# Seven block products for eight in the last channel mixing of a linear-attention and mixer kernel

## Chip, cores and metric

The kernel runs on one core of one Trainium2 chip. The metric is device time in microseconds (us) of one execution; the time of a kernel is the median of several runs.

## What is computed

Attention output of eight batches is the input of a token and channel mixer. Cut to what matters:

```python
# q, k, v: (8 batches, 8 heads, 576 positions, 64)
q_p, k_p = phi(q), phi(k)                       # phi(x) = (x if x > 0 else exp(x) - 1) + 1
kv = einsum('bhsd,bhse->bhde', k_p, v)
num = einsum('bhsd,bhde->bhse', q_p, kv)
den = einsum('bhsd,bhd->bhs', q_p, sum(k_p, axis=2))[..., None] + 1e-06
x = (num / den), as (8, 576, 512)
u = x + (relu(x^T @ w_tok1) @ w_tok2)^T         # token mixing: 576 -> 256 -> 576
out = u + relu(u @ w_ch1) @ w_ch2               # channel mixing: 512 -> 1536 -> 512
```

The change touches the last product, `relu(u @ w_ch1) @ w_ch2`, of the last two batches.

## The kernel before

The 576 positions of a batch are four row tiles of 128 (`R = 4`) and a tail of 64; the tails of two batches (a pair `p`, batches n = 2p and 2p + 1) share one tile of 128. A row tile r holds the positions 9p' + 2r + e: the lower 64 partitions are e = 0, the upper 64 are e = 1, and `outv` sends each half to its own rows of the output.

Each batch goes through these steps:

- `phi` on q and k: ScalarE takes the exponential (L124), VectorE adds (L130) and takes a minimum (L138). `kv` and `nd` form the attention; `nd_end` has VectorE divide (L217, L219, L220).
- `mm1` and `mm2` are the token mixing. `mm2` leaves its product in a PSUM tile `h_ps`, and VectorE adds x to give `u` (L271). `mm2_tails` does so for a pair's tail (L280, L284), giving `ut`. DMA transposes make `uT` and `uTt` of them (L464, L469).
- `mm3` is the first half of the channel mixing: 12 blocks of 128 hidden channels, each of 4 matmuls of 512 columns (L480); ScalarE applies the relu and writes block mc of the bf16 tile `cr[n % 2]` (L487). `mm3_tail` does the same for the tails of a pair, 48 matmuls of 128 columns (L494), into `crt`.
- `mm4` is the second half. A row tile t takes 12 matmuls of 512 columns (L506) into one PSUM bank; `mm4_end` has VectorE add `u` into an output tile `o_sb` (L523, or L533 for the tail tile, t = 8) and starts the transfers to the output (L528, L535).

PSUM has two pools: `ps_big` with four banks of 128 x 512 f32 and `ps_sm` with two tiles of two banks. `o_sb` tiles come from a pool of five.

The order on every engine is written out by hand. The main loop runs over n from 2 to 7. Its list `big` holds the steps of `mm3` (0 to 11), for odd n those of `mm3_tail`, then thirds of `mm4` tiles. The list `fill` says which steps of the next batches are put after which step of `big`: the next batch's kv, nd, mm1, mm2a (row tiles 0 and 1), mm2b (2 and 3) and mm2t (tails) come at the places in `AT`. Each engine works through its queue in this order; a step that waits holds everything behind it on its engine.

For the last pair the outputs are sent from the queues of SP and ACT, one row tile at a time, and for the other pairs from POOL's queue, two row tiles at a time:

```python
last = p == B // 2 - 1
put = nc.sync if last else nc.gpsimd
```

The last row tile of batch 7 is done by `mm4_last` in two parts of 384 and 128 columns (L543), so that the last add (L546) and transfers (L548) are short.

Below, batch 6 and batch 7 are n = 6 and n = 7.

Of the kernel before, what the change touches and what calls it, by code (L numbers as in the profile page):

```python
# [9 lines left out]
FP32 = mybir.dt.float32  # L10
BF16 = mybir.dt.bfloat16
AF = mybir.ActivationFunctionType
ALU = mybir.AluOpType
# [5 lines left out]
def kernel(  # L19
# [20 lines left out]
    nc = tc.nc  # L40

    B, H, S, D = q.shape
    DM = H * D
    DTOK = moe_w_tok1.shape[1]
    DCH = moe_w_ch1.shape[1]
    R = 4
# [7 lines left out]
    NCH = DCH // 128  # L54
# [6 lines left out]
    outp = ctx.enter_context(tc.tile_pool(name="outp", bufs=5))  # L61
    ps_big = ctx.enter_context(tc.tile_pool(name="ps_big", bufs=4, space=bass.MemoryType.PSUM))
    ps_sm = ctx.enter_context(tc.tile_pool(name="ps_sm", bufs=2, space=bass.MemoryType.PSUM))

    def const(name, shape, dt=BF16):
        return consts.tile(shape, dt, name=name, tag=name)
# [6 lines left out]
    wc2 = const("wc2", [128, NCH, DM])  # L73
    identity = const("identity", [128, 128])

    raw = {(nm, b): const(f"{nm}_raw{b}", [128, HP, TD], FP32) for nm in "kvq" for b in range(2)}
# [7 lines left out]
    u = [const(f"u{b}", [128, R, DM]) for b in range(2)]  # L84
    ut = [const(f"ut{i}", [128, DM]) for i in range(2)]
    uT = [const(f"uT{b}", [128, R, NDM, 128]) for b in range(2)]
    uTt = const("uTt", [128, NDM, 128])
    cr = [const(f"cr{b}", [128, NCH, SM]) for b in range(2)]
    crt = const("crt", [128, NCH, 128])
# [6 lines left out]
    half = [slice(0, 64), slice(64, 128)]  # L96
# [11 lines left out]
    def load(nm, n, c, gate=None):  # L108
        src_ = src[nm][n].rearrange("(j a) (p t) d -> (a p) j (t d)", a=2, t=T)
        js = slice(2 * c, 2 * c + 2)  # L110
        return after(nc.sync.dma_start(out=raw[nm, n % 2][:, js], in_=src_[:, js]), gate)
# [7 lines left out]
    live = {}  # L119
# [22 lines left out]
    def phi(nm, n, c):  # L142
        phi_exp(nm, n, 2 * c, 2)
        phi_add(nm, n, 2 * c, 2)
        phi_end(nm, n, 2 * c, 2)
# [49 lines left out]
    def qtr_dma(n):  # L195
        for a in range(2):
            nc.sync.dma_start_transpose(
                out=qT[n % 2][:, 2 * TD * a:2 * TD * (a + 1)].rearrange("p (f s) -> p f s", s=D),
                in_=qp[half[a]].rearrange("p c t i d -> p (c t i d)"))
# [274 lines left out]
    def mm3(n, mc, kjs=range(NDM), dve=False):  # L474
        b = n % 2
        if kjs[0] == 0:
            part_of[mc] = ps_big.tile([128, 512], FP32, name="c_ps", tag="big")
        ps = part_of[mc]
        for kj in kjs:
            nc.tensor.matmul(out=ps, lhsT=wc1[:, kj, 128 * mc:128 * mc + 128],  # L480
                             rhs=uT[b][:, :, kj],
                             start=(kj == 0), stop=(kj == NDM - 1))
        if kjs[-1] == NDM - 1 and dve:
            nc.vector.tensor_scalar(out=cr[b][:, mc, :], in0=ps, scalar1=0.0, scalar2=None,
                                    op0=ALU.max)
        elif kjs[-1] == NDM - 1:
            nc.scalar.activation(out=cr[b][:, mc, :], in_=ps, func=AF.Relu)  # L487

    def mm3_tail(i):
        ps = ps_big.tile([128, 4, 128], FP32, name="c_ps", tag="big")  # L490
        for m in range(4):
            mc = 4 * i + m
            for kj in range(NDM):
                nc.tensor.matmul(out=ps[:, m], lhsT=wc1[:, kj, 128 * mc:128 * mc + 128],  # L494
                                 rhs=uTt[:, kj, :], start=(kj == 0), stop=(kj == NDM - 1))
        nc.scalar.activation(out=crt[:, 4 * i:4 * i + 4, :], in_=ps, func=AF.Relu)
# [3 lines left out]
    def mm4(p, t, kcs, wait=False):  # L500
        if kcs[0] == 0:
            held[t] = ps_big.tile([128, DM], FP32, name="h2_ps", tag="big")
        ps = held[t]
        b, r = divmod(t, R)
        for kc in kcs:
            nc.tensor.matmul(  # L506
                out=ps, lhsT=crt[:, kc, :] if t == 8 else cr[b][:, kc, 128 * r:128 * r + 128],
                rhs=wc2[:, kc, :], start=(kc == 0), stop=(kc == NCH - 1))
        if kcs[-1] == NCH - 1 and not wait:
            mm4_end(p, t)  # L510

    outv = out.rearrange("n (p t) d -> n p t d", t=T)
# [23 lines left out]

    def mm4_last(cs):

        p, b, r = B // 2 - 1, 1, R - 1
        m = cs.stop - cs.start  # L540
        ps = ps_big.tile([128, 512], FP32, name="h2_ps", tag="big")[:, 0:m]
        for kc in range(NCH):
            nc.tensor.matmul(out=ps, lhsT=cr[b][:, kc, 128 * r:128 * r + 128],  # L543
                             rhs=wc2[:, kc, cs], start=(kc == 0), stop=(kc == NCH - 1))
        o = outp.tile([128, 2, DM], FP32, name="o_sb", tag="o_sb")[:, 0, 0:m]
        nc.vector.tensor_tensor(out=o, in0=ps, in1=u[b][:, r, cs], op=ALU.add)  # L546
        for e in range(2):
            (nc.scalar if e else nc.sync).dma_start(out=outv[2 * p + b, :, 2 * r + e, cs],  # L548
                                                    in_=o[half[e]])

    def prep_k(n, g, copy=nc.scalar.copy):
        phi("k", n, g)
        vcast(n, g, copy)

    def load_all(n, nms):
        if n < B:
            for nm in nms:
                for g in range(2):
                    load(nm, n, g)
# [118 lines left out]
    def steps(n):  # L678

        out_ = [("kv", lambda: kv(n, range(2)))]  # L680
        if n == 1:
            puts = [nc.scalar.copy, nc.vector.tensor_copy if n == 1 else nc.scalar.copy]
            out_ += [(f"qt{c}", lambda c=c: qtr(n, c, puts[c])) for c in range(2)]
        for i, rs in enumerate(([0, 1], [2, 3], [4])):
            for g in range(2):
                out_.append((f"nd{i}{g}", lambda g=g, rs=rs: nd(n, g, rs)))
        out_.append(("mm1", lambda: mm1(n)))
        if n > 1:
            out_ += [("mm2a", lambda: mm2(n, [0, 1])), ("mm2b", lambda: mm2(n, [2, 3]))]
            if n % 2:  # L690
                out_.append(("mm2t", lambda: mm2_tails(n // 2)))
            out_ += [("uta", lambda: utr_dma(n, [0, 1])), ("utb", lambda: utr_dma(n, [2, 3]))]
            if n % 2:
                out_.append(("utt", lambda: utr_tail_dma(n // 2)))
        return out_

    def run(bigs, fill):
        for i, big in enumerate(bigs):
            big()
            for s, fn in fill:  # L700
                if s == i:
                    fn()
        for s, fn in fill:
            assert s < len(bigs)

    m3 = lambda n, k0=0: [lambda mc=mc: mm3(n, mc) for mc in range(k0, NCH)]
    m3t = [lambda i=i: mm3_tail(i) for i in range(3)]
    m4 = lambda p, ts: [lambda t=t, i=i: mm4(p, t, range(4 * i, 4 * i + 4))
                        for t in ts for i in range(3)]
# [6 lines left out]
    big = [lambda mc=mc: mm3(0, mc, range(2, 4)) for mc in range(3)] + \  # L716
# [4 lines left out]
    fill = [(2, mm2_first_tail)]  # L721
# [8 lines left out]
    first = steps(1)  # L730
# [12 lines left out]
    big = [lambda mc=mc: mm3(1, mc, range(2, 4)) for mc in range(3)] + [lambda mc=mc: mm3(1, mc, dve=mc in (5, 8)) for mc in range(3, NCH)] + m3t + m4(0, [4, 5, 6, 7, 8])  # L743
    at1 = {"kv": 8, "nd00": 10, "nd01": 11, "nd10": 12, "nd11": 13, "nd20": 14, "nd21": 15,
           "mm1": 17, "mm2a": 19, "mm2b": 20, "mm2t": 21, "uta": 19, "utb": 20}
    fill = [(s, lambda g=g: phi("k", 2, g)) for g, s in ((0, 0), (1, 2))]
# [11 lines left out]
    for n in range(2, B):  # L758
        p, b = divmod(n, 2)
        if b == 0:  # L760
            big = m3(n) + m4(p, [0, 1, 2, 3])
        else:
            big = m3(n) + m3t + m4(p, [4, 5, 6, 7, 8])
            if n + 1 == B:
                big = m3(n) + m3t + m4(p, [8, 4, 5, 6]) + [
                    lambda: mm4_last(slice(0, DM - 128)), lambda: mm4_last(slice(DM - 128, DM))]
        fill = []
        if n + 1 < B:
            fill += [((AT3 if n == 2 else AT)[nm], fn) for nm, fn in steps(n + 1)]
        if n + 2 < B:  # L770
            d = 1 if n == 2 else 0
            fill += [(s + d, lambda g=g: phi("q", n + 2, g)) for g, s in ((0, 8), (1, 9))]
            fill += [(12 + d, lambda: qtr_dma(n + 2))]
            if n == 2:
                fill += [(16, lambda: load_all(5, "qkv"))]
            fill += [(s + d, lambda g=g: prep_k(n + 2, g)) for g, s in ((0, 14), (1, 16))]
            fill += [(18, lambda: load_all(n + 4, "qkv"))]
        run(big, sorted(fill, key=lambda e: e[0]))

# [28 lines left out]
```

## Time and profile before

| what | us |
|---|---|
| median of 8 runs | 262.18 (261.78 to 262.36) |
| the profiled execution, time | 261.78 |
| the profiled execution, span of the core | 260.0 |
| TensorE matmul busy | 251.9 (97% of the span) |
| VectorE busy | 146.2 (56%) |
| ScalarE busy | 130.9 (50%) |
| GpSimd (POOL) busy | 34.9 (13%) |

The span runs from the first to the last event of the core in the trace; the execution's time is longer by what lies around it. "PE" is TensorE's matmul row, "PEld" its weight loads, "DVE" VectorE, "ACT" ScalarE, "POOL" GpSimd, "SP" the SyncE queue. A busy share is a mean over stages with different limits; what a stage is worth is read from its own part of the timeline. The tensor names of the profile leave out numbers: `wc` is `wc1` or `wc2`, and `h_ps` stands also for the bank `h2_ps` of `mm4`.

### The profile page before, as it was taken

To read this page: it belongs to the slowest core of one execution; us is meant where nothing else is said; L and a number is where in the kernel's file an instruction comes from. 1 tells how busy PE (TensorE), PEld (TensorE's weight loads), DVE (VectorE), ACT (ScalarE), POOL (GpSimd) and SP (SyncE) were. 2 spreads that over 40 slices of the span, in tenths; PEclk is the share of its full clock that TensorE was granted. 3 is DMA by queue.
4 is the path that set the end of the run, shared out by engine and by line. 5 is a ranking of instruction groups with operands and counts; after the bars stand their busy time and mean duration, and the time that the engine had idled before them with its cause. 6 is when DMAs were issued, how large, how long until landed. Compare 5 with 4: busy or idle time off the path is not lost.

```text
span 260.0 us, 5043 instructions
## 1 busy us (share of the span) xinstructions
PE 251.9 (97%) x2052; PEld 131.6 (51%) x2070; DVE 146.2 (56%) x283; ACT 130.9 (50%) x205; POOL 34.9 (13%) x58
## 2 busy tenths in 40 slices
PE   7999999999999999999999999999999999999993
PEld 3574465645644554455654544455554554444642
DVE  5875769865966376837662475928563363420122
ACT  4755863387580568146680569236780453036300
POOL 9760210110012100110003200030002300000000
PEclk9999999999999999999999999999999999999999
DMA  7999999999049960899998961760094500930043
GB/s 259 253 204 287 357 212 389 268 266 411 28 105 210 370 237 15 184 259 398 410 277 222 363 244 24 169 156 9 0 147 108 125 0 10 157 98 0 3 104 98
DMA packets 50087, 48.34 MB, mean 186 GB/s; under 512 B 30288, under 2 KB 35536, under 8 KB 50064
## 3 DMA queue, kind: packets, MB, share of 16 engines
q1 hardware_dynamic: 41904, 35.53, 46.0%
q0 software_dynamic: 7440, 11.44, 20.6%
q10 hardware_dynamic: 720, 1.05, 1.1%
q8 instruction: 16, 0.26, 0.4%
q14 instruction: 7, 0.06, 0.1%
HBM read 35.85 MB, written 9.44 MB: 174 GB/s over the span
## 4 chain that ended last, share of the span: by engine, by line
PE 83%; DMA 8%; POOL 3%; ACT 2%; DVE 1%; issue 1%; SPq 0%; POOLq 0%; ACTq 0%
PE h_ps L506 33%; PE c_ps L480 28%; PE a_ps L246 5%; DMA q_raw<-in_q_dram 5%; PE c_ps L494 4%; PE h_ps L259 4%; DMA wc<-in_moe_w_ch_dram 3%; PE nd_ps L208 3%; PE kv_ps L167 2%; PE h_ps L543 1%; ACT e L124 1%; POOL qT L587 1%; POOL cr L116 1%; PE h_ps L280 1%; ACT u L301 0%
## 5 line engine op out<-in xcount | busy, mean ns | idle before, releaser
L487 ACT ACTIVATE cr<-c_ps 128x512 bf16<-128x512 f32 x91 | 53.3, 599 | 77.1 <-PE c_ps L480 77.1
L480 PE MATMUL c_ps<-uT,wc 128*128 128x512 bf16 x384 | 91.5, 379 | 0.0
L506 PE MATMUL h_ps<-wc,cr 128*128 128x512 bf16 x363 | 84.3, 379 | 0.5
L506 PEld LDWEIGHTS <-cr 128*128 128x128 bf16 x372 | 35.6, 98 | 41.8 <-issue 1.2
L480 PEld LDWEIGHTS <-wc 128*128 128x128 bf16 x384 | 35.7, 98 | 36.7 <-issue 1.2
L523 DVE TENSOR_TENSOR o_sb<-h_ps,u 128x512 f32<-128x512 f32 x31 | 21.2, 689 | 24.5 <-PE h_ps L506 24.3
L528 POOL DMA_DIRECT2D out_dram<-o_sb x24 | 14.5, 606 | 149.7 <-DVE o_sb L523 149.5
L220 DVE TENSOR_TENSOR x<-nd_ps,den 128x512 bf16<-128x512 f32 (+1 forms) x42 | 25.3, 602 | 1.4
L124 ACT ACTIVATE e<-q_raw 128x1152 bf16<-128x1152 f32 x16 | 18.5, 1161 | 7.0 <-DMA q_raw<-in_q_dram 7.0
L124 ACT ACTIVATE e<-k_raw 128x1152 bf16<-128x1152 f32 x16 | 18.7, 1170 | 2.4 <-DMA k_raw<-in_k_dram 2.3
L271 DVE TENSOR_TENSOR u<-h_ps,x 128x1024 bf16<-128x1024 f32 x12 | 14.6, 1220 | 9.2 <-PE h_ps L259 9.2
L138 DVE TENSOR_TENSOR qp<-e,y 128x1152 bf16<-128x1152 bf16 x16 | 12.1, 757 | 13.6 <-ACT e L124 13.1
L217 DVE TENSOR_SCALAR den<-nd_ps 128x8 f32<-128x8 f32 (+1 forms) x42 | 6.8, 163 | 19.7 <-PE nd_ps L208 19.0
L138 DVE TENSOR_TENSOR kp<-e,y 128x1152 bf16<-128x1152 bf16 x16 | 12.1, 757 | 8.0 <-ACT e L124 7.4
L208 PEld LDWEIGHTS <-qT 128*128 128x128 bf16 x140 | 11.4, 98 | 9.3 <-issue 0.2
L208 PE MATMUL nd_ps<-kvbd,qT 128*128 128x130 bf16 x140 | 15.1, 223 | 0.0
L246 PE MATMUL a_ps<-x,w 128*128 128x512 bf16 x50 | 13.9, 379 | 0.3
L149 ACT CAST vs<-v_raw 128x1152 bf16<-128x1152 f32 x12 | 13.9, 1161 | 0.0
L533 DVE TENSOR_TENSOR o_sb<-h_ps,ut 128x512 f32<-128x512 f32 x4 | 2.8, 690 | 19.1 <-PE h_ps L506 19.1
L130 DVE TENSOR_SCALAR y<-k_raw 128x1152 bf16<-128x1152 f32 x16 | 12.0, 752 | 1.6 <-DMA k_raw<-in_k_dram 1.5
L130 DVE TENSOR_SCALAR y<-q_raw 128x1152 bf16<-128x1152 f32 x16 | 12.2, 765 | 1.0 <-DMA q_raw<-in_q_dram 1.0
L259 PE MATMUL h_ps<-ar,w2p 128*128 128x512 bf16 x48 | 12.3, 379 | 0.0
(102 smaller groups left out, 203.4 us busy)
## 6 DMA issues: line engine op xcount, KB each, us to landing
k_raw<-in_k_dram SPq DMA_DIRECT2D x16, 576.0 KB, 9.8
q_raw<-in_q_dram SPq DMA_DIRECT2D x16, 576.0 KB, 7.7
v_raw<-in_v_dram SPq DMA_DIRECT2D x14, 576.0 KB, 11.5
out_dram<-o_sb POOLq DMA_DIRECT2D x24, 256.0 KB, 5.0
wc<-in_moe_w_ch_dram POOLq DMA_DIRECT2D x8, 384.0 KB, 9.4
out_dram<-o_sb SPq DMA_DIRECT2D x9, 128.0 KB, 2.3
out_dram<-o_sb ACTq DMA_DIRECT2D x7, 128.0 KB, 2.6
out_dram<-o_sb POOLq DMA_DIRECT2D x6, 128.0 KB, 6.0
```

What stands on the lines that cost most here:

```text
L124: nc.scalar.activation(out=e, in_=f, func=AF.Exp)
L130: nc.vector.tensor_scalar(out=y, in0=f, scalar1=1.0, scalar2=1.0, op0=ALU.add, op1=ALU.max)
L138: nc.vector.tensor_tensor(out=dst.transpose([0, 2, 1, 3]), in0=e.rearrange("p (i t d) -> p i t d", i=nj, t=T), in1=y.rearrange("p (i t d) ...
L208: nc.tensor.matmul(out=o[:, a], lhsT=qT[b][:, t0:t0 + 128], rhs=kvbd[b][:, c, a], start=True, stop=True)
L220: nc.vector.tensor_tensor(out=x[b][:, rs[0]:rs[0] + m, HG * D * g:HG * D * (g + 1)].rearrange("p r (h d) -> p r h d", h=HG), in0=v_[:, :, ...
L246: nc.tensor.matmul(out=ps[:, mt], lhsT=w1t[:, b, ms] if r == R else w1[:, r, ms], rhs=x[b][:, r, :], start=(r == 0), stop=(r == R))
L259: nc.tensor.matmul(out=ps[:, i], lhsT=w2v(kt, r, b), rhs=ar[b][:, kt, :], start=(kt == 0), stop=(kt == NT - 1 and not add))
L271: nc.vector.tensor_tensor(out=u[b][:, rs[0]:rs[0] + m], in0=ps[:, 0:m], in1=x[b][:, rs[0]:rs[0] + m], op=ALU.add)
L480: nc.tensor.matmul(out=ps, lhsT=wc1[:, kj, 128 * mc:128 * mc + 128], rhs=uT[b][:, :, kj], start=(kj == 0), stop=(kj == NDM - 1))
L487: nc.scalar.activation(out=cr[b][:, mc, :], in_=ps, func=AF.Relu)
L506: nc.tensor.matmul(out=ps, lhsT=crt[:, kc, :] if t == 8 else cr[b][:, kc, 128 * r:128 * r + 128], rhs=wc2[:, kc, :], start=(kc == 0), stop ...
L523: nc.vector.tensor_tensor(out=o, in0=ps, in1=u[b][:, r, :], op=ALU.add)
```

## The change

In batches 6 and 7 the product of four row tiles of hidden values with `w_ch2` is done as products of blocks. The two tiles of a pair j of row tiles (2j and 2j + 1) are the block rows (e = 0, 1), the halves of the 1536 hidden channels are the inner blocks, and the halves of the 512 output channels are the block columns. Seven products of blocks (128 x 768 with 768 x 256, six matmuls of 256 columns each) replace eight per pair, in a form with running sums: products 1, 6, 7 and 4 accumulate in one bank X per pair of row tiles, and VectorE reads X after each of them; product 2 has a bank Z; products 5 and 3 accumulate in a tile Y of the pool `ps_sm`.

- `weight_sums` forms differences of blocks of `w_ch2` on POOL: 18 instructions over 512 elements a partition, in three groups of six that stand after steps 18, 19 and 20 of batch 5. They are kept in the raw input buffers of k and q that are no longer needed.
- `row_sums` forms sums of blocks of the hidden values on VectorE: per batch one instruction of 1536 elements and six of 768, after steps 9, 10 and 12. They are kept in the raw buffers of v.
- `product` runs one product for a pair j and the VectorE adds that go with it, in the order `ORDER` of (product, j); seven adds of 256 columns per pair of row tiles replace two of 512.
- The outputs of both batches are sent from POOL's queue, 128 KB each, eight per batch.
- The tail tile of the last pair, which was the first `mm4` tile of batch 7, is now what `mm4_last` does at the end, in the same two parts.

```diff
     def mm4_last(cs):
 
-        p, b, r = B // 2 - 1, 1, R - 1
+        p = B // 2 - 1
...
-            nc.tensor.matmul(out=ps, lhsT=cr[b][:, kc, 128 * r:128 * r + 128],
+            nc.tensor.matmul(out=ps, lhsT=crt[:, kc, :],
...
-        nc.vector.tensor_tensor(out=o, in0=ps, in1=u[b][:, r, cs], op=ALU.add)
-        for e in range(2):
-            (nc.scalar if e else nc.sync).dma_start(out=outv[2 * p + b, :, 2 * r + e, cs],
-                                                    in_=o[half[e]])
+        nc.vector.tensor_tensor(out=o, in0=ps, in1=ut[p % 2][:, cs], op=ALU.add)
+        for b in range(2):
+            (nc.scalar if b else nc.sync).dma_start(out=outv[2 * p + b, :, 2 * R, cs],
+                                                    in_=o[half[b]])
+    KH = NCH // 2
...
+    def weight_sums(k0, m):
+        ks = slice(k0, k0 + m)
+        b11, b12, b21, b22 = [wblock(i, j)[:, ks] for i in range(2) for j in range(2)]
+        sub = lambda o, x_, y_: nc.gpsimd.tensor_tensor(out=o[:, ks], in0=x_, in1=y_, op=ALU.subtract)
+        sub(tf, b12, b11)
+        sub(tb[0], b12, b11)
+        sub(tb[1], b22, tf[:, ks])
+        sub(tb[2], b22, b12)
+        sub(tf, b22, tf[:, ks])
+        sub(tb[3], b21, tf[:, ks])
...
+    def row_sums(n, which, k0, m):
+        ks = slice(k0, k0 + m)
+        a11, a12, a21, a22 = [ablock(n, i, e)[:, ks] for e in range(2) for i in range(2)]
+        x_, y_, op = {1: (a21, a22, ALU.add), 2: (sb[0][:, ks], a11, ALU.subtract),
+                      3: (a11, a21, ALU.subtract), 4: (a12, sb[1][:, ks], ALU.subtract)}[which]
+        nc.vector.tensor_tensor(out=sb[which - 1][:, ks], in0=x_, in1=y_, op=op)
...
+    def product(n, j, i):
+        b, p = n % 2, n // 2
+        a_ = lambda h, e: ablock(n, h, e)[:, :, j]
+        lhs, rhs, tile_, first = {
+            1: (a_(0, 0), wblock(0, 0), "X", True), 2: (a_(1, 0), wblock(1, 0), "Z", True),
+            6: (sb[1][:, :, j], tb[1], "X", False), 5: (sb[0][:, :, j], tb[0], "Y", True),
+            7: (sb[2][:, :, j], tb[2], "X", False), 4: (a_(1, 1), tb[3], "X", False),
+            3: (sb[3][:, :, j], wblock(1, 1), "Y", False)}[i]
...
+        for k_ in range(KH):
+            nc.tensor.matmul(out=ps, lhsT=lhs[:, k_], rhs=rhs[:, k_], start=(first and k_ == 0),
+                             stop=(k_ == KH - 1), skip_group_check=not first)
...
+        if i == 1:
+            add(0, 0, ps, ur(0, 0))
+        elif i == 2:
+            add(0, 0, ps, o[:, 0, HC[0]])
+        elif i == 6:
+            add(0, 1, ps, ur(0, 1))
+        elif i == 7:
+            add(1, 1, ps, ur(1, 1))
+            add(1, 1, live["Y", j], o[:, 1, HC[1]])
+        elif i == 4:
+            add(1, 0, ps, ur(1, 0))
+        elif i == 3:
+            add(0, 1, ps, o[:, 0, HC[1]])
+        if i in (4, 3):
+            d, r = (1 if i == 4 else 0), 2 * j + (1 if i == 4 else 0)
+            for e in range(2):
+                nc.gpsimd.dma_start(out=outv[n, :, 2 * r + e], in_=o[half[e], d])
+
+    ORDER = [(1, 0), (1, 1), (2, 0), (6, 0), (2, 1), (6, 1), (5, 0), (7, 0), (5, 1), (7, 1),
+             (4, 0), (3, 0), (4, 1), (3, 1)]
...
-            big = m3(n) + m4(p, [0, 1, 2, 3])
+            big = m3(n) + (m4s(n) if n + 2 == B else m4(p, [0, 1, 2, 3]))
...
-                big = m3(n) + m3t + m4(p, [8, 4, 5, 6]) + [
+                big = m3(n) + m3t + m4s(n) + [
                     lambda: mm4_last(slice(0, DM - 128)), lambda: mm4_last(slice(DM - 128, DM))]
...
+        if n + 3 == B:
+            fill += [(18 + i, lambda i=i: weight_sums(2 * i, 2)) for i in range(3)]
+        if n + 2 >= B:
+            fill += [(9, lambda n=n: row_sums(n, 3, 0, KH))]
+            fill += [(s, lambda n=n, w=w, k0=k0: row_sums(n, w, k0, 3))
+                     for s, k0 in ((10, 0), (12, 3)) for w in (1, 2, 4)]
```

More of the change, by code (lines that the diff above doesn't have):

```diff
@@ new lines, in mm4_last, with bf @@
+        for b in range(2):
+            (nc.scalar if b else nc.sync).dma_start(out=outv[2 * p + b, :, 2 * R, cs],
+                                                    in_=o[half[b]])
+    KH = NCH // 2
+    def bf(nm, b, i):
+        t = raw[nm, b].rearrange("p j f -> p (j f)").bitcast(BF16)
+        return t[:, 1536 * i:1536 * (i + 1)]
+    tb = [bf("k", 0, i).rearrange("p (k c) -> p k c", k=KH) for i in range(3)] + [
+        bf("q", 0, 0).rearrange("p (k c) -> p k c", k=KH)]
+    tf = raw["q", 0].rearrange("p j f -> p (j f)")[:, 768:2304].rearrange("p (k c) -> p k c", k=KH)
@@ new lines, with wblock @@
+    sb = [(bf("v", 0, i) if i < 3 else bf("v", 1, 0)).rearrange("p (k j s) -> p k j s", k=KH, j=2)
+          for i in range(4)]
+    def wblock(i, j):
+        return wc2[:, KH * i:KH * (i + 1), 256 * j:256 * (j + 1)]
+    def weight_sums(k0, m):
[8 more added lines that the diff above has]
+        sub(tb[3], b21, tf[:, ks])
@@ new lines, in ablock @@
+    def ablock(n, i, e):
+        return cr[n % 2].rearrange("p k (j e s) -> p k j e s", j=2, e=2)[:, KH * i:KH * (i + 1), :, e]
+    def row_sums(n, which, k0, m):
[4 more added lines that the diff above has]
+        nc.vector.tensor_tensor(out=sb[which - 1][:, ks], in0=x_, in1=y_, op=op)
@@ new lines @@
+    HC = [slice(0, 256), slice(256, 512)]
+    def product(n, j, i):
[6 more added lines that the diff above has]
+            3: (sb[3][:, :, j], wblock(1, 1), "Y", False)}[i]
+        if first and tile_ != "Y":
+            live[tile_, j] = ps_big.tile([128, 512], FP32, name="h2_ps", tag="big")[:, 0:256]
+        elif first:
+            live["Y", j] = ps_sm.tile([128, 2, 512], FP32, name="y_ps", tag="sm")[:, 0, 0:256]
+        ps = live[tile_, j]
+        for k_ in range(KH):
+            nc.tensor.matmul(out=ps, lhsT=lhs[:, k_], rhs=rhs[:, k_], start=(first and k_ == 0),
+                             stop=(k_ == KH - 1), skip_group_check=not first)
+        if i == 1:
+            live["oj", j] = outp.tile([128, 2, DM], FP32, name="o_sb", tag="o_sb")
+        o = live["oj", j]
+        ur = lambda e, c: u[b][:, 2 * j + e, HC[c]]
+        add = lambda e, c, x_, y_: nc.vector.tensor_tensor(out=o[:, e, HC[c]], in0=x_, in1=y_,
+                                                           op=ALU.add)
+        if i == 1:
+            add(0, 0, ps, ur(0, 0))
[14 more added lines that the diff above has]
+                nc.gpsimd.dma_start(out=outv[n, :, 2 * r + e], in_=o[half[e], d])
@@ L551, in prep_k, with m4s @@
+    ORDER = [(1, 0), (1, 1), (2, 0), (6, 0), (2, 1), (6, 1), (5, 0), (7, 0), (5, 1), (7, 1),
+             (4, 0), (3, 0), (4, 1), (3, 1)]
+    def m4s(n):
+        return [lambda i=i, j=j: product(n, j, i) for i, j in ORDER]
     def prep_k(n, g, copy=nc.scalar.copy):
```

## The prediction

> **What bounds the kernel now.** I read the page's busy shares, then the chain that ended last, then the timeline of the last 45 us, then the transfers.
>
> ```profile
> span 260.0 us, 5043 instructions
> PE 251.9 (97%) x2052; PEld 131.6 (51%) x2070; DVE 146.2 (56%) x283; ACT 130.9 (50%) x205; POOL 34.9 (13%) x58
> ...
> PE 83%; DMA 8%; POOL 3%; ACT 2%; DVE 1%; issue 1%; SPq 0%; POOLq 0%; ACTq 0%
> ```
>
> TensorE is busy for 97% of the span and is 83% of the chain: work taken from it counts, if nothing else comes to stand in its way. The end of the chain, in order of time (start, us, what):
>
> ```profile
> 224.30 5.78 PE h_ps L506 x26
> 230.07 10.36 PE c_ps L480 x48
> 240.44 2.68 PE c_ps L494 x48
> 243.17 10.31 PE h_ps L506 x47
> 253.47 2.63 PE h_ps L543 x24
> 256.13 0.29 DVE o_sb L546
> ```
>
> 48 matmuls of 512 columns take 10.36, so 215.8 ns each; 48 of 128 columns take 2.68, so 55.8 ns. No gap: batch 7's L506 follows its L494 at once. After the last add (256.42) only four small transfers remain. VectorE in batch 6, from the timeline (start, us, engine and line, output and inputs, count, idle before it):
>
> ```profile
> 218.23 1.22 DVE L271 TENSOR_TENSOR u<-h_ps,x 128x1024 bf16<-128x1024 f32 x1 [5.64 <-PE h_ps L259]
> ...
> 219.96 1.23 DVE L271 TENSOR_TENSOR u<-h_ps,x 128x1024 bf16<-128x1024 f32 x1 [0.50 <-PE h_ps L259]
> ...
> 222.29 1.40 DVE L284 TENSOR_TENSOR ut<-h_ps,x 64x512 bf16<-64x512 f32 x2
> ```
>
> The reader is to see that VectorE already has 3.85 us of adds for batch 7 exactly where the changed stage begins, and they are wide. Last, the transfers that carry outputs (issuer, count, KB each, us from issue to landing), over the whole run:
>
> ```profile
> out_dram<-o_sb SPq DMA_DIRECT2D x9, 128.0 KB, 2.3
> out_dram<-o_sb ACTq DMA_DIRECT2D x7, 128.0 KB, 2.6
> out_dram<-o_sb POOLq DMA_DIRECT2D x6, 128.0 KB, 6.0
> ```
>
> POOL's 6.0 is a median beside input loads. Late and alone (issued at 203.84 and 204.38) the 128 KB pair of L535 still took 3.5 and 3.3.
>
> **What the Trainium skill says.** TensorE: Matmul & The Clock Gate, Back-to-back issue gap: N/2.4 + 2.5 ns, so 109 for 256 columns; the trace's 215.8 and 55.8 agree, and their line gives 109.1, which I use. GPSIMD Engine Reference, section 3.1: a two-input add of 2048 elements takes 4497 ns at some 2.6 cycles an element; my estimate for 512 elements is 1.15 us. No run here shows one. SBUF — State Buffer, Who interferes with whom: a VectorE instruction with two SBUF inputs and a GpSimd one that reads SBUF block each other for a whole instruction, one with a PSUM input and one SBUF input doesn't. The trace of before has no such pair. DMA: Bandwidth & Descriptors, Anatomy of one DMA: about 2.0 us + bytes/436e3 for a GpSimd DMA, 2.3 for 128 KB; here it is 3.3 to 3.5, and the measurement decides.
>
> **1. Matmuls.** Per batch, 4 tiles x 12 matmuls of 512 columns (48 x 215.8 = 10.36) become 14 products x 6 of 256 (84 x 109.1 = 9.17, 0.655 a product): −1.19 per batch, −2.38 in all if TensorE never waits. The smaller matmuls keep their weight loads hidden: the 128-column ones of L494 do at 55.8. Bounds on the rate: 108 to 115, so −2.6 to −1.4.
>
> **2. Weight sums on POOL.** 18 subtractions, 1.15 each by the estimate, 20.7. In POOL's queue twelve stand behind the output issues that end near 173.2, so they run to about 187 to 190; six stand behind L528's at 196.07 to 197.27 and end near 204.5. They push the outputs of batch 5 (L528, 201.25; L535, 203.84) back by some 3 us; nobody waits for those. TensorE first needs a sum at 221.4. VectorE's phi adds and minima (L130, L138) of 180.6 to 194.5 may be blocked by up to one POOL instruction each; five of them start before 190, 5 x 1.15 = 5.8 at most. Behind them are batch 7's q and k, batch 6's u (ready at 189.3 now, used by TensorE from 202.7) and the output adds, the first of which ends at 195.06 while its bank is needed again at 200.07. I count zero; the bounds are 0 and 1.
>
> **3. Row sums on VectorE.** Adds from PSUM cost 158 + 1.04 ns an element (L220: 692 for 512, 425 for 256). L138, bf16 in SBUF, takes 757 for 1152; with the same 158 that is 0.52 an element. So the 1536 form costs 0.96 and the 768 form 0.56; at the full rate per element, 1.75 and 0.96. In batch 6 the first four (0.96 + 3 x 0.56 + gaps = 2.8) fit VectorE's idle 212.6 to 218.2. The last three, because they need hidden blocks 9 to 11, are queued behind both u adds.
>
> **4. The queue in batch 6.** VectorE's order becomes u, add (1,0), u, three sums, adds (1,1) and (2,0), two ut adds (0.69 each), add (6,0). With 0.04 between instructions, from 218.23: 219.45, 219.92, u 219.95 to 221.17, sums to 221.77, 222.37, 222.97, adds to 223.43 and 223.90, ut to 224.62 and 225.35, add (6,0) to 225.81. TensorE from 218.03: (1,0), L259, (1,1), (2,0), L280 end at 221.41. Product (6,0) does three matmuls and waits for the second half of the second sum (222.37, and 0.27 to load and start): it resumes at 222.64, 0.90 late. (2,1), (6,1), (5,0) end at 224.93. (7,0) accumulates on the bank that add (6,0) reads, so it starts at 225.87, 0.94 late. From there each wait is met: (4,0) needs an add that ends at 227.20 and starts at 227.84. Stall 1.84; the stage changes by −1.19 + 1.84 = **+0.65**. If the sums run at the full rate per element it is 1.2 more.
>
> **5. Batch 7.** VectorE is idle between 231 and 245 now, so all sums are done beforehand and the same walk has no stall: −1.19. The tail tile goes last in place of a row tile, with the same 24 matmuls (2.63). The last matmul is thus 0.54 earlier than before, and so are the adds at 255.9 and their four SP and ACT transfers. By that path the span is 259.46.
>
> **6. The outputs.** Batch 6 and 7 now send 16 transfers of 128 KB from POOL, and SP and ACT lose theirs. In batch 6 nothing waits for them. In batch 7 the products start at 243.6 (L543's 253.31 in the timeline − 10.36 + 0.65). The add of (4,0) ends 8.10 later at 251.70; POOL issues 0.29 after (L533's end 203.55 to L535's 203.84), at 251.99. The other three rows are ready by 253.4, sooner than POOL gets to them: 8 issues at 0.54 (L535: 539 ns), the last at 255.77. Lower bound: it lands after 3.4, at 259.17. Upper bound: 768 KB issued by POOL between 201.25 and 204.38 had landed by 207.68, 6.43 from the first issue; 1024 KB at that rate take 8.57, so 260.56. The middle is 259.87, and the four last transfers (256 KB, about 1.0 at the 257 GB/s that POOL's queue had in its own share of 203.7 to 214) share the engines: I take 260.1. Now the last transfer is issued at 256.6 and lands after 2.2, at 258.8; the span ends 1.2 later. So the span becomes 261.3, **+1.3**. This transfer is late next where TensorE was.
>
> The profiled execution took 261.78, 1.78 above its span; the median of 8 runs is 0.40 above that. 261.3 + 1.78 + 0.40 gives **263.5**.
>
> **Rivals.** **A, POOL's outputs land early** (faster): if the last lands by 258.3, 2.5 after its issue, the SP and ACT path sets the end: 262.18 − 0.54 = 261.6, and 259.8 if batch 6 doesn't stall either. For it: the issues are spread over 3.8 us. Against: none of the six outputs that POOL issued after 196 landed in under 3.0. It decides from 0.8 less than the lower bound of step 6. Chance 0.16. **B, the row sums run at the full rate**, or a POOL sum is late at 221.4: 1.2 more at the stall moves batch 7 and its outputs alike, 264.7. For it: the sums read strided halves. Against: L138 has a strided output and keeps the rate. POOL's 18 sums would have to take 2.7 us each to reach from 173.2 to 221.4. Chance 0.18. **C, POOL blocks VectorE in batch 5** so long that TensorE waits: up to +1, 264.5; the slack named in step 2 speaks against it. 0.06. **The forecast** has 0.60, of which 0.12 lies at its lower bound, where the span is 260.4 and the time within 0.2% of before. That it doesn't do what it says is excluded: the instruction order shows the 168 matmuls, 18 and 14 sums and 16 transfers.
>
> **The numbers.** A measurement of this kernel can tell about 0.2% (0.52) from no change. Slower 0.72 (0.48 + 0.18 + 0.06), same 0.12, faster 0.16. The range 261.7 to 265.0 leaves out A and the worst of B.
>
> **What would show it.** Right: 168 matmuls of 256 columns near 109 ns apart; TensorE idle for some 0.9 twice near 222 and 225 with VectorE as the releaser, and L480 of batch 7 starting 0.65 later; no idle in batch 7's products; POOL's last output issue near 255.8, after the last add of a row, landing after SP's and ACT's. Wrong: batch 6's stage shorter than 11.9, POOL's last landing within 2.5 of its issue, or 768-element sums that take 0.96.

## Result and profile after

The changed kernel takes **264.05 us** (median of 11 runs, 263.42 to 264.48) against 262.24 for the kernel before, run in turn with it: a ratio of 1.0062, 95% interval 1.0053 to 1.0072. The forecast of 263.5 was 0.55 short, its sign and range held. The profiled execution took 263.70, with a span of 261.9 against 260.0.

The page after, its span, its busy shares and the engines' shares of the chain that ended last:

```profile
span 261.9 us, 5233 instructions
PE 249.9 (95%) x2126; PEld 138.7 (53%) x2142; DVE 161.9 (62%) x317; ACT 130.9 (50%) x205; POOL 65.9 (25%) x92
...
PE 83%; POOL 5%; DVE 3%; DMA 3%; issue 2%; ACT 2%; POOLq 0%; DVEq 0%
```

TensorE has 2.0 us less work, and the span is 1.9 longer. The chain no longer ends in VectorE's last add; it leaves TensorE at 249.9, 12 us before the end, for three adds and POOL (start, us, what):

```profile
230.27 10.36 PE c_ps L480 x48
240.63 2.68 PE c_ps L494 x48
243.31 3.93 PE h_ps L605 x36
...
254.00 1.05 POOL out_dram L629 x2
255.04 0.52 POOLq L895
```

L629 are POOL's output issues of batch 7; L895 is the end of the program. A DRAIN is one of the closing instructions there. The view of that line gives engine, operation, count, shortest/median/longest ns, first and last start. Before, where the line is L803, and after:

```profile
L803 POOLq DRAIN  x3: 51/93/5284, 204.3 to 259.7; - x3
L803 SPq DRAIN  x3: 7/7/7, 259.2 to 259.5; - x3
```

```profile
L895 POOLq DRAIN  x3: 51/102/6466, 254.7 to 261.6; - x3
L895 SPq DRAIN  x3: 7/7/13, 259.7 to 261.4; - x3
```

POOL's first DRAIN stands behind its last output issue and takes 5.3 us before and 6.5 after (its record begins up to 1.0 us before that issue does, so below only its end counts). Before, it ran from 204.3 to 209.6, with 50 us to spare; now it runs from 254.7 to 261.1. SP has its last landing and reaches its own first DRAIN at 259.7, then waits: the engines meet in a barrier that needs POOL. The waits of SP's queue (us in total, times, longest) say the same; the second stood at 0.7, 2, 0.5 before:

```profile
SPq L895 <- DMA out_dram<-o_sb: 2.9, 2, 2.7
SPq L895 <- PEq L895: 2.0, 2, 1.5
```

The view names TensorE's queue, since it puts a wait for several signals down to the one that came last. But TensorE, VectorE and ScalarE had ended their first DRAINs by 257.0, and the next DRAIN of every engine starts between 261.3 and 261.5, just after the end of POOL's at 261.1: POOL is what held the barrier.

The transfers in the last 11 us (issuer, count, KB each, us from issue to landing). First the four short ones of before, then those of after:

```profile
out_dram<-o_sb SPq DMA_DIRECT2D x1, 96.0 KB, 2.1
out_dram<-o_sb ACTq DMA_DIRECT2D x1, 96.0 KB, 2.4
out_dram<-o_sb SPq DMA_DIRECT2D x1, 32.0 KB, 2.1
out_dram<-o_sb ACTq DMA_DIRECT2D x1, 32.0 KB, 2.2
```

```profile
out_dram<-o_sb POOLq DMA_DIRECT2D x8, 128.0 KB, 3.0
out_dram<-o_sb SPq DMA_DIRECT2D x1, 96.0 KB, 3.8
out_dram<-o_sb ACTq DMA_DIRECT2D x1, 96.0 KB, 4.0
out_dram<-o_sb SPq DMA_DIRECT2D x1, 32.0 KB, 3.5
out_dram<-o_sb ACTq DMA_DIRECT2D x1, 32.0 KB, 3.7
```

Batch 6 and batch 7 as stretches, from the first product to what follows the last (stretch; length, then busy us and count of each engine, clock, DMA share, GB/s):

```profile
218.46:230.11 11.65, 11.03 (x94) 8.57 (x92) 10.23 (x20) 0.00 (x0) 0.91 (x2) 1.00 0.42 58
243.15:252.32 9.17, 9.17 (x88) 8.21 (x85) 5.42 (x13) 0.60 (x1) 0.92 (x2) 1.00 0.00 0
```

Batch 7's products take 9.17 without a gap. Batch 6's take 11.65, where the same stretch before (218.03 to 229.91) took 11.88.

The span's 1.9 thus has five terms. Batch 6 brings −0.23 and batch 7 −1.19. This profile ran 0.43 late before the changed stages began (batch 6's L480 starts at 203.09, before at 202.66); over all the profiles of this study that start lies between 202.66 and 203.56, and in the two kernels below that have no block product it lies at 203.03 and 203.32, so this term is not the change's. From the start of L543 to SP's DRAIN 7.41 pass instead of 5.86, +1.55, because the last four landings are slower. POOL's DRAIN ends 1.41 after SP reached its own, where it had ended long before. The sum is +1.97, against 1.93 measured.

### The profile page after: what moved, and what is told of

Its sections match the earlier page's. It is cut to its first block, busy times and chain, and to the rows that moved or that the text cites. A ratio compares the mean times of both kernels' runs of the same rounds, so it can differ in the third digit from the quotient of the medians.

```text
span 261.9 us, 5233 instructions
## 1 busy us (share of the span) xinstructions
PE 249.9 (95%) x2126; PEld 138.7 (53%) x2142; DVE 161.9 (62%) x317; ACT 130.9 (50%) x205; POOL 65.9 (25%) x92
## 4 chain that ended last, share of the span: by engine, by line
PE 83%; POOL 5%; DVE 3%; DMA 3%; issue 2%; ACT 2%; POOLq 0%; DVEq 0%
PE c_ps L480 32%; PE h_ps L506 25%; PE a_ps L246 5%; PE c_ps L494 4%; PE h_ps L259 4%; PE nd_ps L208 3%; DMA w<-in_moe_w_tok_dram 3%; PE h_ps L605 3%; PE kv_ps L167 2%; PE y_ps L605 1%; POOL out_dram L629 1%; POOL w2p L451 1%; DVE o_sb L611 1%; POOL qT L673 1%; POOL cr L116 1%
## 5 line engine op out<-in xcount | busy, mean ns | idle before, releaser
L480 PE MATMUL c_ps<-uT,wc 128*128 128x512 bf16 x384 | 91.4, 379 | 0.0
L506 PE MATMUL h_ps<-wc,cr 128*128 128x512 bf16 x280 | 65.5, 379 | 0.5
L480 PEld LDWEIGHTS <-wc 128*128 128x128 bf16 x384 | 35.8, 98 | 36.4 <-issue 1.4
L528 POOL DMA_DIRECT2D out_dram<-o_sb x24 | 14.5, 609 | 130.4 <-DVE o_sb L523 130.1
L506 PEld LDWEIGHTS <-cr 128*128 128x128 bf16 x288 | 27.5, 98 | 31.6 <-issue 0.8
L523 DVE TENSOR_TENSOR o_sb<-h_ps,u 128x512 f32<-128x512 f32 x24 | 16.4, 688 | 13.2 <-PE h_ps L506 13.0
L629 POOL DMA_DIRECT2D out_dram<-o_sb x16 | 8.3, 528 | 40.4 <-DVE o_sb L611 40.4
L130 DVE TENSOR_SCALAR y<-q_raw 128x1152 bf16<-128x1152 f32 x16 | 13.6, 850 | 0.2 <-DMA q_raw<-in_q_dram 0.2
```

The lines of the kernel that those rows point to most:

```text
L130: nc.vector.tensor_scalar(out=y, in0=f, scalar1=1.0, scalar2=1.0, op0=ALU.add, op1=ALU.max)
L506: nc.tensor.matmul(out=ps, lhsT=crt[:, kc, :] if t == 8 else cr[b][:, kc, 128 * r:128 * r + 128], rhs=wc2[:, kc, :], start=(kc == 0), stop ...
L523: nc.vector.tensor_tensor(out=o, in0=ps, in1=u[b][:, r, :], op=ALU.add)
```

## Experiments

The theory from the two traces: POOL's closing DRAIN comes due about 5.5 us after POOL's last output issue and now ends the program. The rival: the memory traffic of eight late 128 KB outputs ends it, whoever issues them. A second question was why batch 6 lost 0.96 (11.65 against the 11.88 of before less 1.19) and not the 1.84 of the prediction.

### Batch 7's outputs from SP and ACT

```diff
-                nc.gpsimd.dma_start(out=outv[n, :, 2 * r + e], in_=o[half[e], d])
+                q_ = nc.gpsimd if n + 1 < B else nc.scalar if e else nc.sync
+                q_.dma_start(out=outv[n, :, 2 * r + e], in_=o[half[e], d])
```

> The changed kernel with the eight outputs of batch 7 sent from SP (e = 0) and ACT (e = 1) instead of POOL; batch 6 still sends from POOL. Theory D: what ends the changed kernel is POOL's closing DRAIN, which ends some 5.6 us after the end of POOL's last output issue (issue ends at 255.56, drain at 261.14) and holds the closing barrier. Without late POOL outputs it ends near 239 and the barrier waits for the last landing, as before: last adds 0.99 earlier than before in the profiled runs, so a span near 259.0 and 261.1 us, 1.0 to 1.2 faster than before. Rival B (the forecast's step 6): the end is late because eight POOL transfers back up on the DMA engines; in the profile the last landing is only 0.55 later than before, so at most that much is won, 263.5 us.

Measured: 261.17 us, ratio to the kernel before 0.9964 (0.9951 to 0.9977), span 259.3. In the view of the program's last line:

```profile
L896 POOLq DRAIN  x3: 51/102/5303, 232.3 to 259.0; - x3
L896 SPq DRAIN  x3: 7/7/13, 258.5 to 258.8; - x3
```

The DRAIN still lasts 5.3 us, but from 232.3, and SP's at 258.5 is not kept waiting. The same bytes leave in the last microseconds, and 2.9 us are gone: what the changed kernel paid for hung on the issuer, not on the amount of traffic. In the two profiles the spans differ by 2.6: 1.4 is the wait for POOL's DRAIN, 1.1 the shorter stretch from L543 to SP's DRAIN (6.33 for 7.41) and 0.2 an earlier start, less 0.1 at the very end. The middle term need not be POOL's nature: POOL issued its eight outputs from 251.40 to 255.56, SP and ACT had begun theirs by 253.2, and these runs don't part the two. With the outputs on SP and ACT the change is a gain.

### Batch 6's outputs too

The same line with `q_ = nc.scalar if e else nc.sync`.

> The changed kernel with all sixteen outputs of batches 6 and 7 sent from SP and ACT. Theory D: as after_hw7 within 0.2 us (261.1), because batch 6's POOL outputs end 20 us before the end. If late POOL outputs cost something by themselves in batch 6 (descriptor making beside VectorE's adds, or shared engines), this is faster than after_hw7 by more than 0.3. If the ACT issues, which stand in ScalarE's queue ahead of batch 7's relu, delay it, it is slower by 0.3 or more.

Measured: 261.32 us, ratio 0.9968 (0.9959 to 0.9978). No difference from the last run that these runs can tell: POOL's outputs at 229 to 233 cost nothing here.

### Half of batch 7's outputs

The same line with `q_ = nc.gpsimd if n + 1 < B or j == 0 else nc.scalar if e else nc.sync`.

> Only the last four outputs of batch 7 (second pair of row tiles) go to SP and ACT; the first four stay on POOL, whose last issue then ends about 253.4 in the changed kernel's clock instead of 255.6. Drain theory: the closing DRAIN ends 4.4 to 5.6 after that issue, at 257.8 to 259.0, before SP has its last landing (about 258.4 to 259.2), so at most 0.6 above all eight on SP and ACT: 261.2 to 261.8. Rival (transfers share the engines, and any of POOL's among them delays the last landings): half of the gain, 262.6.

Measured: 262.03 us, ratio 0.9998 (0.9988 to 1.0008): between the two expectations.

```profile
L896 POOLq DRAIN  x3: 51/93/6987, 252.7 to 260.2; - x3
L896 SPq DRAIN  x3: 7/7/7, 258.8 to 260.0; - x3
```

The mechanism holds, my length didn't. POOL's last issue ended at 253.45, as expected, but the DRAIN ended at 259.7, 6.3 later, and 0.9 after SP's; the time is 0.86 above that of the first experiment. POOL's four outputs landed in 4.0 here, not 3.0, so the DRAIN's end goes with the landing of POOL's data more than with its issue.

### The kernel before with late POOL outputs

First, row tile 6's two outputs of 128 KB from POOL (`nc.gpsimd if last and t == 6` in L528):

> The kernel before with the two transfers of its row tile 6 (batch 7, r = 2; 128 KB each, issued at 254.2 from SP and ACT) sent from POOL. Same bytes, same matmuls, two POOL issues from 254.5 to 255.6. Theory D: POOL's drain ends near 261.2 instead of 209.6, the barrier two us later: 264.0 to 264.4. Rival B (only a backlog of transfers counts): two transfers land within 3.5 us of their issue, before the last SP and ACT ones at 258.8: 262.2, no change.

Measured: 262.60 us, ratio 1.0012 (1.0005 to 1.002). Much less than expected: with two outputs in flight POOL's data was down at 257.6 and the DRAIN at 259.9, only 0.2 after SP's 259.7. Second, the two final outputs of 32 KB from POOL:

```diff
-            (nc.scalar if e else nc.sync).dma_start(
+            (nc.gpsimd if cs.start else nc.scalar if e else nc.sync).dma_start(
```

> The kernel before with only the two final 32 KB outputs (the last 128 columns of row tile 7) issued by POOL: it issues them about 256.0 and 256.5, ending 257.1. Drain theory: DRAIN ends 4.0 to 4.7 later, at 261.1 to 261.8, against 259.2 for the kernel before: 264.1 to 264.8 us, ratio 1.007 to 1.010. Rival (only the landing counts; a POOL landing takes 2.4 to 3.0): last landing 259.5 instead of 258.85, then 262.9.

Measured: 264.87 us, ratio 1.0100 (1.0086 to 1.0115), in a kernel without a single block product:

```profile
L803 POOLq DRAIN  x3: 51/102/4533, 257.8 to 262.9; - x3
L803 SPq DRAIN  x3: 7/7/13, 260.2 to 262.6; - x3
```

The two outputs landed in 1.9 us, where SP's and ACT's of 32 KB took 2.1 and 2.2 before, and the kernel is 2.6 us slower all the same. A slow landing can't be the cause. In the profile, whose span is 3.1 longer, POOL's DRAIN ends 2.1 after SP reached its own. The rest is a start of batch 6 that is 0.7 late, and POOL's later issues, 0.3 and 0.8 after the last add. The seven profiles together, in us:

| kernel | POOL's last issue ends | POOL's last packet ends | POOL's DRAIN ends | SP reaches its DRAIN | span |
|---|---|---|---|---|---|
| before | 204.9 | 207.2 | 209.6 | 259.2 | 260.0 |
| after | 255.6 | 258.3 | 261.1 | 259.7 | 261.9 |
| batch 7 from SP and ACT | 233.2 | 235.0 | 237.6 | 258.5 | 259.3 |
| half from SP and ACT | 253.5 | 256.6 | 259.7 | 258.8 | 260.5 |
| new order in batch 6 (below) | 254.4 | 257.0 | 259.9 | 258.5 | 260.7 |
| before, row tile 6 from POOL | 255.9 | 257.6 | 259.9 | 259.7 | 260.7 |
| before, last 32 KB from POOL | 258.4 | 259.3 | 262.3 | 260.2 | 263.1 |

In every row the span ends 0.8 after the later of the two DRAIN columns. The DRAIN ends 2.3 to 3.1 after POOL's last packet (2.2 to 3.1 over all thirteen profiles of this study), and 3.9 to 6.3 after the end of its last issue. What it does in those 2 to 3 us no view shows.

### The order in batch 6

```diff
+        if n + 2 == B:
+            at = {"mm2b": 13, "utb": 13, "mm2t": 25, "utt": 25}
+            fill = [(at[nm], fn) for nm, fn in steps(n + 1) if nm in at] + [
+                ((AT)[nm], fn) for nm, fn in steps(n + 1) if nm not in at]
...
+            fill += [(s, lambda n=n, w=w, k0=k0: row_sums(n, w, k0, 3))
+                     for s, w, k0 in ((10, 1, 0), (10, 2, 0), (10, 4, 0), (11, 1, 3), (11, 2, 3), (17, 4, 3))]
```

The late halves of sums 1 and 2 go ahead of the second u add, that add after (1,1) and (2,0) have started, and the tails to the stage's end. Outputs stay on POOL.

> The changed kernel with VectorE's order in batch 6 changed alone: the late halves of row sums 1 and 2 come straight after the first u add, mm2b one step later, the late half of sum 4 after product (6,1), the tail's mm2t (with its ut adds) after the last product. Outputs stay on POOL. Theory: the 0.96 us that TensorE loses in batch 6 (waits for sums 2 and for add (6,0)) goes, everything after it moves up by 0.7 to 1.0, POOL's issues and its drain too: 263.1 to 263.3. Rival: the stall is cover for something else (the uT transposes of batch 7, one step later here, or batch 7's sums), then the time stays at 264.0.

Measured: 262.85 us, ratio 1.0023 (1.0016 to 1.0031), 1.2 below the changed kernel. The stage is down from 11.65 to 10.74. In the timeline VectorE now has the sums between the two u adds, and adds that nothing delays start 0.33 apart:

```profile
218.37 1.23 DVE L271 TENSOR_TENSOR u<-h_ps,x 128x1024 bf16<-128x1024 f32 x1 [3.12 <-PE h_ps L259]
219.51 0.55 DVE L587 TENSOR_TENSOR v_raw<-cr 128x768 bf16<-128x768 bf16 x1
220.09 0.56 DVE L587 TENSOR_TENSOR v_raw<-v_raw,cr 128x768 bf16<-128x768 bf16 x1
...
222.36 0.41 DVE L611 TENSOR_TENSOR o_sb<-h_ps,o_sb 128x256 f32<-128x256 f32 x1
222.69 0.41 DVE L611 TENSOR_TENSOR o_sb<-h_ps,u 128x256 f32<-128x256 f32 x1
```

So the queue of VectorE was the cause of the stall: with the same instructions in another order 0.91 of the 0.96 are gone.

### The form in batch 7 alone

Batch 6 keeps `m4(p, [0, 1, 2, 3])` and its outputs; batch 7 has the products, with outputs from SP and ACT.

> Batch 6's channel mixing as in the kernel before, Strassen's form in batch 7 alone, its outputs on SP and ACT. By my corrected sum batch 6's form brings 1.19 - 0.96 (wait) = 0.23, so without it 261.4 us, 0.2 above the kernel with both (261.17). The prediction's stall of 1.84 would have made batch 6 a loss of 0.65, so without it 260.5. Rival: batch 6's row sums also delay what follows, by an amount that only shows here: under 260.8.

Measured: 260.97 us, ratio 0.9956 (0.9944 to 0.9968). That is 0.2 below the kernel with both batches changed (261.17), not 0.2 above, and the intervals overlap, so batch 6's form in the order of the change is worth nothing that these runs can tell. The stage did lose its 0.23 (11.88 again), but the end is shorter: from TensorE's DRAIN to SP's 4.9 pass, as in the kernel before, where the kernel with both took 5.3. The 128 KB outputs differ in the same way: 2.7 and 3.3 us to landing here, 4.1 and 4.3 there. In the transfer records of the latter, and of the other kernels so far with the form in both batches, an instruction queue (q8) fetches 16 KB at 251.5 to 253.7, for 0.9 to 1.6 us; here its last fetch is at 244.5. That it is TensorE's queue, and that it matters, the next runs test.

### Both edits, and the fetch moved

Outputs of batch 7 from SP and ACT, with the new order in batch 6:

> Both edits together: batch 7's eight outputs issued by SP and ACT, and the changed order of VectorE's and TensorE's work in batch 6. Drain theory and order effect are separate, so the gains add: 264.05 - 2.9 (outputs) - 1.2 (order) = 260.0 us, ratio about 0.992. Rival: the order only filled a wait that the late end hid in part, so the two overlap: 260.8 to 261.2, no better than the outputs alone.

Measured: **260.59 us**, ratio 0.9934 (0.9922 to 0.9945), 1.7 below the kernel before. The order brought 1.2 on the changed kernel and 0.6 here; these differences are uncertain by 0.3 and by 0.5, and the stage's 0.91 lies between. Then the four float32 warm-up matmuls of the start are replaced by 64 bfloat16 ones, in this kernel and in the changed one:

```diff
-    warm(4)
+    warm_bf(64)
```

> As the kernel with both edits (260.59 us), but the four float32 warm-up matmuls of the start are replaced by 64 bfloat16 ones, which adds 127 instructions to TensorE's stream (0.055 us of matmuls per instruction in the last stage), so that TensorE's 16 KB instruction fetch seen at 252.75 moves to about 246, ahead of the last outputs. Fetch theory (a fetch of 0.95 us on the transfer engines delays the outputs in flight, 128 KB landing in 4.1 instead of 2.7 us, the end 0.45 later): 128 KB landings back to about 2.7 to 3.3, 260.1 us. Rival (the slower landings come from something else in the order of the transfers): landings stay at 4.1 and the time at 260.6.

> The changed kernel with the same addition at the start: TensorE's instruction fetch at 252.58 moves to about 246. If the fetch also holds up POOL's transfers, POOL's DRAIN, which waits for them, ends up to 0.5 earlier: 263.5 to 263.7 us. If the DRAIN has a length of its own behind POOL's last issue, nothing changes: 264.0.

Measured: 260.36 us, ratio 0.9926 (0.9912 to 0.9939), and 264.14, ratio 1.0067 (1.0055 to 1.008). The last fetch moved to 245.9 and 246.8. In the first kernel the outputs answered as the fetch theory said. The transfers at the end with both edits, and with the fetch moved as well:

```profile
out_dram<-o_sb SPq DMA_DIRECT2D x4, 128.0 KB, 4.1
out_dram<-o_sb ACTq DMA_DIRECT2D x4, 128.0 KB, 4.2
```

```profile
out_dram<-o_sb SPq DMA_DIRECT2D x4, 128.0 KB, 2.7
out_dram<-o_sb ACTq DMA_DIRECT2D x4, 128.0 KB, 3.4
```

From TensorE's DRAIN to SP's it is 4.9 instead of 5.3. Over the kernels with batch 7's outputs on SP and ACT it is 5.3 to 5.4 in the four profiles with a late fetch and 4.9 in the two without. The time doesn't show it: 260.36 and 260.59 can't be told apart, and in the profile batch 6's L480 began 0.55 later (203.52), inside the spread of these profiles, so whether the new warm-up costs that stays open. In the changed kernel SP's and ACT's last landings stayed at 3.4 to 3.9 and the time where it was: there the fetch is not what slows them, and the DRAIN ends it anyway. POOL's first three outputs did land sooner, in 2.3 to 2.6 instead of 3.0 to 3.3, but its last took 3.5 as before (3.6), so this run doesn't decide between the two readings of the DRAIN in its expectation.

### Weight sums twice

In the kernel with both edits, `sub(tb[0], …)` and `sub(tb[2], …)` stand twice in each third.

> As the kernel with both edits (260.59 us), with two of the six weight sums of each third done twice: six more POOL subtractions of 1.15 us, some 6.9 us more work on POOL between 187 and 212. My theory (POOL's sums cost nothing: TensorE waits for none of them): 260.4 to 260.8. Rival (their use of the port that VectorE shares slows phi's operations until TensorE is late): 261 to 262.

Measured: 260.35 us, ratio 0.9923 (0.9904 to 0.9942). Six more sums, 6.9 us of POOL's time between 173 and 208, cost nothing that these runs can tell; the difference from 260.59 is uncertain by some 0.6.

## Why the prediction held, and where not

**Steps 1 and 5 held to the hundredth.** 84 matmuls were to take 9.17; batch 7 takes 9.17, with no stall. Step 5's last add came 0.99 earlier, not 0.54; without this profile's late start of 0.43 it is 1.42, and the difference of 0.88 is step 4's.

**Step 2 held.** The weight sums took 1.14 to 1.17 each where undisturbed and up to 1.72 beside VectorE; phi's additions on q rose from 765 to 850 ns in the mean. The cost of zero was argued from slack. Six more sums cost nothing measurable, and batch 6's L480 started no later (203.09) than in two kernels without sums (203.03 and 203.32). **Step 3 held:** 0.56 for 768 elements, 0.95 for 1536. That takes away rival B; rival C goes with step 2.

**Step 4 failed in size.** The mechanism and the places are those of the text: TensorE waits for the second sum, and (7,0) for add (6,0).

```profile
221.94 0.22 PEld L605 LDWEIGHTS <-v_raw 128*128 128x128 bf16 x3 [0.41 <-DVE v_raw L587]
222.51 0.23 PEld L605 LDWEIGHTS <-v_raw 128*128 128x128 bf16 x3 [0.36 <-DVE v_raw L587]
...
225.05 0.42 DVE L611 TENSOR_TENSOR o_sb<-h_ps,u 128x256 f32<-128x256 f32 x1
225.53 0.82 PE L605 MATMUL h_ps<-k_raw,v_raw 128*128 128x256 bf16 x6 [0.54 <-DVE o_sb L611]
```

The first pause, 0.41, is no stall: before the change the weight loads pause 0.41 behind L280 too. The other two are the forecast waits, but (6,0) loses 0.27 and not 0.90, and (7,0) 0.7 and not 0.94. The whole stall is 0.96, not 1.84, so the stage is 0.23 shorter, not 0.65 longer; that it is shorter than 11.9 is one of the prediction's own signs of being wrong. The wrong term is the 0.04 between VectorE instructions: one that doesn't depend on the one in front starts before that one ends (adds of 0.42 start 0.33 to 0.34 apart; the add behind a u of 1.22 starts after 1.15; the add behind the last sum of 0.56 after 0.48), and the queue gains on the sum at nearly every step. Only dependent ones stand apart as I took all (sums of 0.56 start 0.59 apart). At the end of add (6,0) VectorE was 0.77 ahead of the walk (225.47, where the walk and the late start give 226.24), which is nearly all of the 0.88. The Trainium skill has a part of this (VectorE: DVE Perf Modes, The DRAIN you can't avoid: a next instruction that is not held starts earlier), though what it calls held is not what depends on a result; the prediction didn't use it.

**Step 6 named the right engine and the wrong event.** POOL's outputs of batch 7 set the end, and its last issue began at 255.03 (forecast 255.77; the forecast was later above all because of its longer stall). But POOL's last landing was not last of all: it came at 258.6, before SP's and ACT's four at 258.9 to 259.4, against the forecast 260.1. What stood in its place is not in the prediction at all: the DRAIN that POOL has to finish before the barrier, 1.41 after SP reached its own, and SP's and ACT's short transfers, slowed from 2.1 to 2.4 us to 3.5 to 4.0. Without the DRAIN, by the 0.8 of the table, the span would have ended near 259.7 + 0.8 = 260.5. The constant "the span ends 1.2 after the last landing" was read from a kernel in which POOL had finished 50 us earlier; the profile of before has that DRAIN, 5.3 us long, in the view of the program's last line, which the prediction didn't use. The good total is thus in part luck: what follows the last matmuls was to grow by 1.84 (1.3 + 0.54) and grew by 2.96 (1.55 + 1.41), and the stall that was 0.88 too long made up for most of that. **Rival A** fell with the same step: POOL's last output landed 0.3 after the 258.3 that it asked for, 3.6 after its issue, and the DRAIN ended 2.5 after that landing. With the same 2.5 behind 258.3 it would have ended at 260.8, still after SP's 259.7.

The same section of the Trainium skill says of the DRAINs that the runtime puts before and after a program that they take "~12 ns constant" on all engines. Whether the DRAINs of L895 are of that kind it doesn't say. SP's took 7 to 13 ns; POOL's first took 4.5 to 7.0 us in the kernels here and TensorE's first 1.8, so for them the figure doesn't hold. Of a GpSimd transfer the Trainium skill (Perfetto Trace Analysis, DMA Instruction — SWDGE (GPSIMD)) says that the profile's end of the instruction is that of writing descriptors, not of moving data; this agrees: after, POOL's last issue ends at 255.6 and its last packet at 258.3.

## What to carry over

An engine that is idle in the last stage is not free there: what it must still finish after its last instruction counts to the end of the program, so look at the closing instructions of each engine before giving one of them late work. Here late outputs belonged on SP and ACT: POOL's DRAIN ended up to 6.3 us after POOL's last issue, so that issue had to end about as long before SP reached its own DRAIN. And walk a VectorE queue with the start-to-start distances of the trace, dependent and independent ones apart, not with durations and a gap: the stall came out at twice its size.

## What the runs showed of the hardware

- POOL's closing DRAIN ended 2.2 to 3.1 us after its last packet in all thirteen profiles, and the span ended some 0.8 after the later of it and SP's first DRAIN; two outputs of 32 KB cost 2.6 us (1.0%) by being issued from POOL last.
- TensorE's instruction fetches of 16 KB held up outputs in flight: 128 KB from SP took 4.1 us (median of four) with a fetch beside them and 2.7 without, and the stretch from TensorE's DRAIN to SP's 5.3 and 4.9; the median times didn't show it. Adding 127 TensorE instructions moved the fetch 6 to 7 us earlier; seven products for eight in both batches put one among the last outputs.
- SP's and ACT's short outputs were slower behind late outputs of POOL: the 32 KB took 3.5 to 3.7 us with eight of POOL's before them, 2.7 to 2.8 with four, 2.1 to 2.2 with two, 2.0 to 2.2 with none. Whether POOL as such does it, or that its outputs are issued later and nearer to them, stays open.
